# Issuing the products of y of an attention unit as one run on TensorE

## Chip, cores and metric

One core of one Trainium2 chip. The metric is the device time of one execution in microseconds, the median of the runs. The engines are TensorE (PE), VectorE (DVE), ScalarE (ACT), GpSimd (POOL) and SyncE (SP), which issues most of the DMAs.

## What is computed

A linear recurrence per batch (4) and head (8) over 768 steps with head size 48, and behind it an expert layer on its output:

```python
for t in range(S):
    S_re, S_im = a_re*S_re - a_im*S_im + k v^T, a_re*S_im + a_im*S_re   # a normalised to |a| <= 0.999
    y[:, :, t] = q @ S_re
x = y as (3072 tokens, 384)
act = x @ w_skip > 0;  e = argmax(x @ w_gate);  g = its softmax weight
out = x + g * (relu(x @ w1[e]) @ w2[e])  for the tokens with act, else x
```

All in float32; F = 1024, 8 experts.

## The kernel before

The sequence is cut into 6 chunks of 128 steps, two chunks to a group (3 groups). Three kinds of work run beside each other up to about 360 us:

- `gates` and `chain`: DVE forms the running products W of the normalised `a`, step by step (L413 and L422), for both chunks of a group at once. This is one long dependent chain on DVE and ends with the third group.
- `consumers` (`consume`, `final`): from W they scale q and k. This needs sums on PE (L496) of squares made by ACT (L482), logarithm and exponential on ACT (L503, L504), and several DVE steps (L506 to L514); `trans` turns the results on PE (L629), ACT copies them (L636). The second group is spilled to DRAM and turned back later by `turn` (PE L568, ACT L570). `wfinal` turns the state of W at the end of a group (ACT L642 and L644, PE L647, ACT L649).
- `units`: one unit per chunk c and batch b, written (c,b), 24 in all. `unit_at` multiplies k with q on PE (`pa`, L687). `unit` masks this on DVE into `at` in two halves of four heads (L710, the second is `at_ins`). For c > 0 there is a state from the chunk before: DVE makes RX (L721, L722 or L725), PE sums it (L736, L737) and ACT copies it into `Sb`, the tile `st` (L739); in chunks 4 and 5 DVE makes `st` instead (L733). Then PE adds k v^T for the next state (L746), which ACT (L753) or DVE (L751) copies into T, read by the unit of the next chunk and the same batch.

The output y of a unit is `py`, one PSUM bank (the pool has one buffer): for each of four pairs of heads, two products of `vt_` with `at` (L757) and, for c > 0, two products of `Sb` with q (L760) accumulated onto them. Each product gives 64 output partitions and is two PE instructions in the profile, so a unit with a state has 32, one without 16. ACT copies `py` into `yT` (L763), PE turns it and computes the router's scores in the same product (`px`, L771), ACT copies this to `xa` and `lg` (L778 to L789), SP stores `xa` (L793). The routing (`route`, `route1`) is done on DVE with small PE products; POOL scatters the tokens by expert (L865).

The experts (`moe`) follow from about 362 us: for each expert a first layer (L1177), ACT and DVE steps (L1179, L1180) and a second layer (L1209 to L1211), while the weights of the next expert are loaded (L1090) and split (L1101, L1102).

The order of instructions on each engine is not the order of the source. `Order` interleaves the generators above with estimated costs to get a program order; the framework's scheduler then simulates the engines and, whenever one is free, gives it the ready instruction with the lowest number in program order. A `with self.tc.high_priority(offset=n)` makes the number of what it holds smaller by n. `issue_after` keeps an instruction behind another on its own engine; `behind` adds a dependency with a wait. On the chip each engine runs its instructions in the order so fixed.

Of the kernel before, what the change touches and what calls it, by code (L numbers as in the profile page):

```python
# [19 lines left out]
B, H, S, D = 4, 8, 768, 48  # L20
# [19 lines left out]
BIG = float(1 << 20)  # L40
NEAR, ENDS = 2, 3 * LP


P_SOON, P_UNIT, P_ROUTE, P_CONSUME, P_REST, P_GATE, P_WEIGHTS = 0.4, 0.5, 0.7, 1, 1, 2, 3

# [67 lines left out]
class Kern:  # L113
# [99 lines left out]
            nc.sync.dma_start(self.xs[k * ZR:(k + 1) * ZR].rearrange("(n p) d -> p n d", p=128),  # L213
                              self.z.rearrange("p (o d) -> p o d", o=1).to_broadcast([128, ZR // 128, XW]))

    def behind(self, ins, others):

        dep = mybir.DependencyInfo(mybir.DependencyClass.Sync, mybir.DependencyReason.DATA)
        for x in others:
            self.tc.add_manual_dep(ins, x.name, dep, reason="rows of the token tables")  # L220


    def load(self, g, dst, src3, side, j0, n, off, eng=None):
# [472 lines left out]
    def unit(self, c, b):  # L696
        nc = self.nc
        V, A, PE = nc.vector, nc.scalar, nc.tensor
        nm = f"{c}_{b}"
        vt_ = self.vts[(c * B + b) % len(self.vts)]  # L700
        KT, QT = self.kqt.pop((c, b))
        o = self.order
        at = self.un.tile([128, H, C], F32, name=f"at_{nm}", tag="at")
# [26 lines left out]
        if c > 0:  # L730
            Sb = self.sts[(c * B + b) % len(self.sts)]
# [20 lines left out]
            else:  # L752
                A.copy(self.T[b], ps)  # L753
        py = self.ps_y.tile([128, H // 2, C], F32, name=f"py_{nm}", tag="py")
        for hp in range(H // 2):
            for j in range(2):
                PE.matmul(py[j * 64:j * 64 + 64, hp], vt_[:, 2 * hp + j], at[:, 2 * hp + j], start=True, stop=(c == 0))  # L757
            if c > 0:
                for j in range(2):
                    self.py_ins[b] = PE.matmul(py[j * 64:j * 64 + 64, hp], Sb[:, 2 * hp + j], QT(2 * hp + j),  # L760
                                               start=False, stop=True).ins
        yT = self.un.tile([128, H // 2, C], F32, name=f"yT_{nm}", tag="yT", bufs=1)
        self.yT_ins = A.copy(yT.rearrange("p a (k t) -> p a k t", k=2),  # L763
                             py.rearrange("p a (k t) -> p a k t", k=2)[:, :, :, ::-1]).ins
# [21 lines left out]
        ins = A.copy(xa[:, 0:DM].rearrange("p (a k) -> p a k", k=2 * D), px[:, :, 0:2 * D]).ins  # L786
# [645 lines left out]
```

## Time and profile before

| | |
|---|---|
| median of 3 runs | 508.67 us (508.4 to 509.84) |
| profiled execution | 510.8 us, span 509.1 us |
| busy in the span: PE, DVE, ACT, POOL | 424.7, 401.3, 302.7, 97.7 us |
| mean granted clock of PE | 0.895 |
| instructions at L757 and L760 | 384 and 320 |

Durations below come from the profiled execution, whose span leaves 1.7 us of its time outside. In a timeline a row is one group of equal instructions in a row on an engine: start, length from the first start to the last end, engine, line, operation, output and inputs, shapes, count. Since PE instructions are pipelined, the time that a group takes of PE is read from its start to the start of the next group.

### The profile page before, as it was taken

The numbers are of one execution on the slowest core, as the hardware profiler recorded it, in microseconds if no ns is written. First come the engines' busy times: TensorE is split into PE (matmuls) and PEld (weight loads), VectorE is DVE, ScalarE is ACT, GpSimd is POOL, SyncE is SP. The second block draws the span as 40 slices with busy tenths as digits, with TensorE's granted clock in tenths as the row PEclk, the third lists the DMA queues.
The fourth block names the chain that finished last, engine by engine and source line by source line (L and its number), as shares of the span: only waits on it lengthen the run. The fifth ranks groups of instructions, "written<-read, shape, count | busy, mean of one in ns | idle before, by whom it ended". The sixth has DMA issues, their size and how long they took to land. (4 is left out here: it accounts for less than half of the span.)

```text
span 509.1 us, 10059 instructions
## 1 busy us (share of the span) xinstructions
PE 424.7 (83%) x3294; PEld 370.8 (73%) x3294; DVE 401.3 (79%) x1009; ACT 302.7 (59%) x702; POOL 97.7 (19%) x170
## 2 busy tenths in 40 slices
PE   0345556399899878699999999999999999999992
PEld 0234324269786658478888889988989999999992
DVE  3899897989999599699899965888778666776630
ACT  5768777665567566486799663333547454755420
POOL 4011111011212222035100120333301211221111
PEclk9966655579999755799999999999999999999998
DMA  5557877588889797677786518676798667765300
GB/s 96 114 110 155 210 168 169 122 206 210 205 196 224 180 219 165 158 158 198 171 183 162 125 50 262 155 209 179 219 293 269 200 212 258 231 184 198 107 22 27
DMA packets 163457, 88.83 MB, mean 174 GB/s; under 512 B 136923, under 2 KB 156876, under 8 KB 163399
## 3 DMA queue, kind: packets, MB, share of 16 engines
q1 hardware_dynamic: 156087, 71.30, 56.0%
q0 software_dynamic: 6224, 16.63, 11.6%
q8 instruction: 28, 0.46, 0.4%
q10 hardware_dynamic: 1088, 0.20, 0.2%
q14 instruction: 30, 0.25, 0.2%
HBM read 63.39 MB, written 26.58 MB: 177 GB/s over the span
## 5 line engine op out<-in xcount | busy, mean ns | idle before, releaser
L413 DVE TENSOR_TENSOR X<-W,ain 128x192 f32<-128x192 f32 x192 | 67.8, 353 | 3.5 <-ACT ain L339 0.2
L496 PE MATMUL sw<-ws,ident 128*128 128x384 f32 x84 | 46.0, 687 | 29.3 <-ACT ws L482 29.3
L1102 DVE TENSOR_TENSOR l<-r,h 128x768 fp32r<-128x768 f32 (+1 forms) x53 | 56.5, 1072 | 12.4 <-ACT h L1101 12.3
L1179 ACT ACTIVATE hh<-ph 128x240 fp32r<-128x240 f32 x64 | 23.8, 374 | 54.6 <-PE ph L1177 54.6
L1101 ACT CAST h<-r 128x768 fp32r<-128x768 f32 (+1 forms) x53 | 49.1, 935 | 8.2 <-DMA r<-in_moe_w_dram 8.0
L422 DVE TENSOR_TENSOR W<-X 128x96 f32<-128x96 f32 x192 | 48.7, 254 | 3.6
L1177 PE MATMUL ph<-xh,l 128*128 128x240 f32 x192 | 51.2, 275 | 0.0
L496 PEld LDWEIGHTS sw<-ws,ident 128*128 128x128 f32 x84 | 20.1, 262 | 42.4 <-ACT ws L482 31.4
L1177 PE MATMUL ph<-xh,h 128*128 128x240 f32 x192 | 49.9, 275 | 0.1
L1177 PE MATMUL ph<-xl,h 128*128 128x240 f32 x192 | 49.5, 276 | 0.2 <-DVE xl L1131 0.2
L629 PE MATMUL tp<-ident,iw 128*96 128x128 f32 x128 | 24.0, 340 | 28.1 <-DVE iw L514 24.1
L636 ACT COPY qk<-tp 96x256 f32<-96x256 f32 x128 | 39.6, 369 | 8.9 <-PE tp L629 8.7
L1209 PE MATMUL po<-h,hh 128*120 128x384 f32 x128 | 43.5, 340 | 0.5 <-ACT hh L1179 0.4
L1210 PE MATMUL po<-l,hh 128*120 128x384 f32 x128 | 42.9, 337 | 0.0
L629 PEld LDWEIGHTS tp<-ident,iw 128*96 128x96 f32 x128 | 18.5, 159 | 33.0 <-issue 10.8
L757 PE MATMUL py<-at,vt 128*64 128x128 f32 x384 | 41.1, 285 | 1.3 <-DMA vt<-in_v_dram 1.3
L1211 PE MATMUL po<-h,hl 128*120 128x384 f32 x128 | 41.1, 342 | 0.0
L710 DVE TENSOR_TENSOR at<-pa,mask 128x512 f32<-128x512 f32 x48 | 32.2, 683 | 8.4 <-PE pa L687 6.4
L687 PE MATMUL pa<-qk 96*128 96x128 f32 x256 | 35.5, 286 | 2.5 <-DVE at L710 2.4
L687 PEld LDWEIGHTS pa<-qk 96*128 96x128 f32 x256 | 31.5, 194 | 6.8 <-DVE at L710 3.5
L1177 PEld LDWEIGHTS ph<-xh,l 128*128 128x128 f32 x192 | 36.4, 190 | 0.0
L1180 DVE SCALAR_TENSOR_TENSOR hl<-ph,hh 128x240 fp32r<-128x240 f32 x64 | 25.7, 402 | 13.5 <-ACT hh L1179 13.3
(254 smaller groups left out, 1075.8 us busy)
## 6 DMA issues: line engine op xcount, KB each, us to landing
r<-in_moe_w_dram SPq DMA_DIRECT2D x24, 512.0 KB
r<-in_moe_w_dram SPq DMA_DIRECT2D x32, 384.0 KB
kq<-nw POOLq DMA_DIRECT2D x24, 192.0 KB, 3.5
kq<-iw POOLq DMA_DIRECT2D x24, 192.0 KB, 3.7
vt<-in_v_dram SPq DMA_DIRECT2D x24, 192.0 KB
out_dram<-xa SPq DMA_DIRECT2D x24, 192.0 KB
nat<-kq SPq DMA_DIRECT2D x6, 768.0 KB
ain<-in_a_im_dram SPq DMA_DIRECT2D x90, 48.0 KB
```

What stands on the lines that cost most here:

```text
L413: V.tensor_tensor(X, prev.unsqueeze(1).to_broadcast([128, 2, 2, D]), windows(ain[:, j]), ALU.mult)
L422: self.cins = V.tensor_tensor(W[:, j, ::-1], X[:, :, 0], X[:, :, 1], ALU.add).ins
L496: nc.tensor.matmul(sw, self.ident, ws[:, :, c], start=(c == 0), stop=(c == 1))
L629: nc.tensor.transpose(tp[:, jj], src[:, s * 4 + jj], self.ident)
L687: nc.tensor.matmul(pa[h // 4][:, h % 4], KT(h), QT(h), start=True, stop=True)
L757: PE.matmul(py[j * 64:j * 64 + 64, hp], vt_[:, 2 * hp + j], at[:, 2 * hp + j], start=True, stop=(c == 0))
L1101: nc.scalar.copy(hi[:, ks], raw)
L1102: nc.vector.tensor_tensor(lo[:, ks], raw, hi[:, ks], ALU.subtract)
L1177: pe = PE.matmul(ph, w[:, k, js], x[:, k], start=(n == 0), stop=(n == len(terms) - 1))
L1209: PE.matmul(po, hh[:, j, sl], w2h[:, j], start=(j == 0), stop=False)
L1210: PE.matmul(po, hh[:, j, sl], w2l[:, j], start=False, stop=False)
L1211: pe = PE.matmul(po, hl[:, j, sl], w2h[:, j], start=False, stop=(j == NF - 1))
```

## The change

In a unit with a state the order of the four pairs of heads is reversed, the state products of a pair come ahead of its products with `at`, and the first of them is made to wait for the second half of `at` by an added dependency. All products of y, also those of chunk 0, get a priority 400 instructions earlier. `behind` takes a reason as an argument.

```diff
+YPRIO = 400
...
-    def behind(self, ins, others):
+    def behind(self, ins, others, why="rows of the token tables"):

         dep = mybir.DependencyInfo(mybir.DependencyClass.Sync, mybir.DependencyReason.DATA)
         for x in others:
-            self.tc.add_manual_dep(ins, x.name, dep, reason="rows of the token tables")
+            self.tc.add_manual_dep(ins, x.name, dep, reason=why)
...
         py = self.ps_y.tile([128, H // 2, C], F32, name=f"py_{nm}", tag="py")
-        for hp in range(H // 2):
-            for j in range(2):
-                PE.matmul(py[j * 64:j * 64 + 64, hp], vt_[:, 2 * hp + j], at[:, 2 * hp + j], start=True, stop=(c == 0))
-            if c > 0:
-                for j in range(2):
-                    self.py_ins[b] = PE.matmul(py[j * 64:j * 64 + 64, hp], Sb[:, 2 * hp + j], QT(2 * hp + j),
-                                               start=False, stop=True).ins
+        with self.tc.high_priority(offset=YPRIO):
+            for hp in range(H // 2) if c == 0 else reversed(range(H // 2)):
+                terms = [(vt_, lambda h: at[:, h])] + ([(Sb, QT)] if c > 0 else [])
+                terms.reverse()
+                for n, (w, x) in enumerate(terms):
+                    for j in range(2):
+                        h = 2 * hp + j
+                        self.py_ins[b] = PE.matmul(py[j * 64:j * 64 + 64, hp], w[:, h], x(h),
+                                                   start=(n == 0), stop=(n == len(terms) - 1)).ins
+                        if c > 0 and n == j == 0 and hp == H // 2 - 1:
+                            self.behind(self.py_ins[b], [self.at_ins], "the unit's products run together")
```

## Rows read from the trace of the kernel before

**Rows 1.** Windows by stretch: length, busy us per engine (instructions), PEclk, DMA share, GB/s.
```profile
110.00:176.00 66.00, 62.33 (x549) 52.38 (x548) 58.53 (x140) 38.05 (x84) 12.51 (x21) 0.95 0.86 212
...
211.00:228.00 17.00, 16.07 (x147) 13.34 (x146) 16.60 (x59) 12.70 (x32) 4.25 (x5) 1.00 0.79 174
228.00:298.00 70.00, 70.00 (x611) 57.30 (x610) 63.71 (x162) 55.53 (x139) 13.20 (x20) 1.00 0.69 157
298.00:362.00 64.00, 62.98 (x693) 57.70 (x692) 48.23 (x172) 23.73 (x62) 16.95 (x18) 1.00 0.67 189
362.00:501.00 139.00, 137.20 (x1003) 135.75 (x1001) 93.06 (x162) 70.12 (x131) 22.65 (x25) 1.00 0.62 192
```

The engines in these rows are, in this order, PE, PEld, DVE, ACT and POOL.

**Rows 2.** Waits of PE from 228 to 362 us: total, times, longest.
```profile
PE px L771 <- ACT yT L763: 0.6, 1, 0.6
PE pa L687 <- DVE at L710: 0.3, 1, 0.3
```

**Rows 3.** Timelines of DVE and PE: end of the recurrence, transpose of its end state.
```profile
297.82 0.25 DVE L422 TENSOR_TENSOR W<-X 128x96 f32<-128x96 f32 x1
...
309.86 0.38 PE L647 MATMUL tpe<-ident,e 128*96 128x128 f32 x2
```

**Rows 4.** Timeline of PE: products ahead of the first and the last break.
```profile
215.94 0.44 PE L757 MATMUL py<-at,vt 128*64 128x128 f32 x4
...
329.31 0.44 PE L757 MATMUL py<-at,vt 128*64 128x128 f32 x4
```

**Rows 5.** Timeline of PE: products, transposes and an unbroken run, with their successors.
```profile
250.87 1.06 PE L687 MATMUL pa<-qkT 96*128 96x128 f32 x8
251.76 0.60 PE L629 MATMUL tp<-ident,iw 128*96 128x128 f32 x4
...
289.71 0.60 PE L629 MATMUL tp<-ident,iw 128*96 128x128 f32 x4
290.15 1.31 PE L746 MATMUL ps<-vt,nat 128*96 128x48 f32 x14
...
341.33 0.44 PE L757 MATMUL py<-at,vt 128*64 128x128 f32 x4
...
343.24 1.16 PE L687 MATMUL pa<-qk 96*128 96x128 f32 x8
```

**Rows 6.** Timeline of PE: broken runs in units (3,2) and (4,1).
```profile
293.86 0.32 PE L757 MATMUL py<-at,vt 128*64 128x128 f32 x1
...
294.88 0.64 PE L629 MATMUL tp<-ident,nw 128*96 128x128 f32 x4
295.45 0.44 PE L757 MATMUL py<-at,vt 128*64 128x128 f32 x4
...
296.48 1.08 PE L568 MATMUL tu<-ident,nat 128*96 128x128 f32 x8
...
322.84 0.44 PE L757 MATMUL py<-at,vt 128*64 128x128 f32 x4
323.20 1.16 PE L687 MATMUL pa<-qk 96*128 96x128 f32 x8
324.30 0.44 PE L760 MATMUL py<-qk,st 96*64 96x128 f32 x4
...
325.98 1.56 PE L746 MATMUL ps<-vt,nat 128*96 128x48 f32 x16
```

**Rows 7.** Timeline of DVE: a step behind the sums of L496, with the idle before it.
```profile
274.02 0.56 DVE L506 TENSOR_TENSOR ws<-sw,ws 128x384 f32<-128x384 f32 x1 [0.65 <-ACT ws L504]
```

**Rows 8.** Windows of PE alone: length, busy us (instructions), PEclk, DMA share, GB/s.
```profile
164.00:166.00 2.00, 0.66 (x8) 1.00 0.67 140
166.00:168.00 2.00, 2.00 (x19) 0.67 1.03 260
168.00:170.00 2.00, 2.00 (x19) 0.50 0.73 188
...
172.00:174.00 2.00, 2.00 (x5) 0.62 0.93 236
```

## The prediction

> **What bounds the kernel now.** I read the windows by stretch first. From 228 to 298 us TensorE (PE) is busy for all 70.00 us and VectorE (DVE) for 63.71; from 298 to 362 PE is busy 62.98 of 64 us and DVE only 48.23; from 362 to 501, in the expert part, PE is busy 137.20 of 139 us [rows 1]. So from 228 us on the work queues for PE. Between 110 and 176 us DVE with the recurrence is nearly full (58.53 of 66), and PE has gaps, so PE time saved there need not reach the end [rows 1].
>
> Busy time of PE is not proof, since ends of matmuls are modelled. So I read the waits of PE second: from 228 to 362 us it waits 0.9 us in all, on two occasions [rows 2]. Third, the end of the recurrence against PE's queue: the last W is made at 297.82 us, and the transpose of the chunk's end state (tpe, L647), which needs only two ScalarE (ACT) copies of it, is run by PE at 309.86 [rows 3]. PE is about 12 us behind at that point; whatever it saves before is saved at the end, up to that lag. What starts at 362 us starts earlier by as much: the experts' work on PE follows without a gap, and its weight loads are released by that work's own copies.
>
> Fourth, how y's products lie on PE. A unit with a state (chunks 1 to 5, 20 units) has 32 PE instructions for y, 16 at L757 and 16 at L760. In the last four units they are one run. In earlier ones the first pair of heads' L757 products come early, then other work, then the rest, and into the rest transposes (L629, L568) fall. Counted on the PE timeline from 211 us, the breaks inside such runs are, unit by unit: 1, 1, 3, 2 (chunk 2), 2, 3, 2, 2 (chunk 3), 1, 1, 1, 0 (chunk 4), none in chunk 5: 19, the first after the products of 215.94, the last after those of 329.31 [rows 4].
>
> **What a break costs.** An unbroken run of 32 takes 343.24 - 341.33 = 1.91 us to the start of what follows, 0.06 us each [rows 5]. Four L629 transposes among full-width work take 290.15 - 289.71 = 0.44 us, eight products at L687 251.76 - 250.87 = 0.89 [rows 5]. Now a broken one: 14 products, four transposes and 16 products take 296.48 - 293.86 = 2.62 us [rows 6]. Thirty products at 0.06 are 1.79, the transposes 0.44; the break costs 0.39. Another: four products, eight of L687 and 28 products take 325.98 - 322.84 = 3.14 us [rows 6], against 1.91 + 0.89; the break costs 0.34.
>
> The Trainium skill, page TensorEngine Tiling (Array Packing), section Tiling Modes, says that changing the tiling mode drains TensorE. That would be one drain out of the half-width products and one back per break, and nothing else. The rows carry more than the two switches: after a switch the first steps of the following group are longer too, so I count the whole stretch, as above, and not the switches alone.
>
> **The change, part by part.** *Order within the run.* State product first, pairs of heads backwards: as many instructions, the same operands, the same sizes. Zero. *Hold.* The first state product also waits for the second mask product of DVE (L710). Nothing of y can then be issued while a factor is missing, so the early pair vanishes. *Priority.* The run ranks 400 instructions earlier, some two units, counting what a unit and the recurrence beside it issue, so the scheduler should put it whole onto PE at the moment that both factors are there, and transposes, L746, L687 and the sums of L496 wait up to 1.91 us longer. No DMA is added or moved by itself; the stores of xa and the scatters behind px follow their unit, so on SyncE's and GpSimd's queues nothing changes its order except by that.
>
> *What it removes.* Of the 19 breaks I leave out the two of units (2,0) and (2,1), since PE was not full before 228 us (16.07 of 17) [rows 1]. Of the other 17, 11 are around transposes, at 0.39, and 6 around L746 or L687, at 0.34: 4.3 + 2.0 = 6.3 us. The four breaks of chunk 1 lie before 176 us, where DVE is the cover: zero, at most 4 x 0.39 = 1.6.
>
> *What it adds.* Standing at the head of PE's queue just when its inputs should be ready, the run can make PE wait for a late DVE or ACT, with everything behind it waiting too. The trace has no such wait for a held run. The nearest row is px (L771), which the scheduler already puts right behind the ACT copy that it needs: 15 of them from 228 to 362 us wait 0.6 us together [rows 2], 0.04 each. For 16 units from chunk 2 on this is 0.6 us. Below: zero. Above: each as long as the one long wait of px, 16 x 0.6 = 9.6 us. I take 0.6 us, as the same kind of step in the same stretch.
>
> *What is late next.* L746 and with it the copy of T: T is read four units later, no loss. For chunk 0 (priority without hold) the first half of the products may run before the second: at most 0.39 in each of two more units, under DVE's cover, zero. The tail of chunk 5 has no break; there only px of one unit and y of the next change places, and PE is full either way.
>
> *Can the other engines follow?* From 228 to 298 us DVE has 63.71 us of work; of its 6.29 idle some is waiting for PE, so some 4 us of shortening nearly fill it, and PE's lag of 12 us [rows 3] carries what DVE cannot.
>
> **Sum.** -6.3 + 0.6 = -5.7 us. The profiled execution took 510.8 us (span 509.1), 2.1 above the median of three runs; it would come to 505.1. On the median, 508.67 - 5.7 = **503.0 us**.
>
> **Rivals.** *Only the tail counts (no measurable change).* If DVE and not PE sets the pace up to the end of the recurrence, or the scheduler still lets older transposes into the runs, then of the savings only the part after 298 us, or only the early pairs, remain. After it are 5 breaks ((3,3) two, (4,0) to (4,2) three): 1.8 - 0.6 = 1.2, **507.5**. For it: DVE at 63.71 of 70 us [rows 1]. Against: PE's lag. If the runs stay broken except for the early pairs, 6 x 0.34 - 0.6 = 1.4, 507.3, the same case.
>
> *The boosted run holds up the recurrence (slower).* In chunks 1 to 3 the sums of L496 and the products of L687 stand behind y by up to 1.91 us; DVE's order is fixed, so a late sum stops the recurrence behind it. The trace has such a wait: L506 idles 0.65 us for ACT's copy behind L496 [rows 7]. One more of these in each of 12 units costs 7.8 us against 5.7 gained: **510.8**. The break-even is 0.48 us per unit, and from 0.6 it is slower by more than 0.3%. For: DVE is nearly full up to 298 us, and the scheduler's times are not the chip's. Against: 12 us of lag on PE mean that L496 already waits its turn there, and DVE has other work.
>
> *The clock falls (smaller gain).* At 164 to 166 us PE was busy 0.66 of 2.00 us; the granted clock was 1.00 there, then 0.67, 0.50 and, in 172 to 174, 0.62, while PE was busy throughout [rows 8]. That is about 6.8 us at half clock (1.2 instead of 2.4 GHz), 3.4 us lost. A hold that leaves PE idle for so long could do it once between 228 and 362: 503.0 + 3.4 = **506.4**. Against: the waits of 0.6 and 0.3 us left the clock at 1.00 from 298 to 362 [rows 1, 2]. The Trainium skill, TensorE: Matmul & The Clock Gate, section on oscillation, warns of the same: gaps between bursts throttle the array, which speaks against holding products back; the trace agrees at 164 us and shows no fall for short waits.
>
> **How the numbers follow.** A measurement of this kernel can tell about 0.3% from no change: 507.1 to 510.2. Forecast 0.54, clock 0.06, tail only 0.17, held-up recurrence 0.23. So faster 0.60, same 0.17, slower 0.23. The low end takes all 19 breaks and the 4 of chunk 1 at 0.39 and no waits: 508.7 - 9.0 = 499.7. The high end takes in the slower rival, 511.0. Beyond it lie the upper bound of the waits (508.67 - 6.3 + 9.6 = 512.0) and larger shifts of order; I leave them and the low side with under 0.2.
>
> **What would show it.** Right: y's products are single runs of 32 of about 1.9 us, state product first, in all 20 units; the stretch from the third unit of chunk 2 to the first L1177 shortens by over 5 us; PE's waits there stay under 2 us; 362 to 501 keeps its length. Wrong: runs still broken; new PE waits on DVE L710 or ACT's copy of the state; the last W later than 297.8 us; a granted clock under 1.00 after 211 us. If the runs are whole and the stretch no shorter, PE was not the bound there. If PE's stretch shortens and the experts start no earlier, routing or weights took its place.

## The result and the profile after

The changed kernel takes 515.68 us in the median (514.52 to 523.31, 4 runs), the one before 508.53 us beside it on the same chip: **1.0128 times as long, 95% interval 1.0095 to 1.0162**. The ratio leaves out the run of 523.31 us, in a slower state into which some executions fall whatever the kernel. The forecast was 503.0 us. 515.68 lies above the range as well.

What the change says, it does: y's products lie on TensorE (PE) as one run of 32 instructions, state product first, in all 20 units with a state. The stretches after, to be held against [rows 1], have PE, PEld, DVE, ACT and POOL in that order behind the length, then the granted clock:

```profile
110.00:176.00 66.00, 60.02 (x554) 50.66 (x554) 62.64 (x153) 41.15 (x91) 16.00 (x29) 0.97 0.87 214
211.00:228.00 17.00, 14.54 (x113) 10.59 (x111) 16.93 (x58) 9.07 (x24) 1.29 (x3) 0.90 0.64 145
228.00:298.00 70.00, 69.08 (x639) 59.12 (x640) 61.44 (x159) 56.77 (x143) 15.10 (x22) 1.00 0.69 162
298.00:362.00 64.00, 59.19 (x643) 55.44 (x642) 44.49 (x145) 21.89 (x57) 14.85 (x16) 0.95 0.61 173
```

PE was full from 298 to 362 us before; now it idles 4.8 of 64 us there, at a mean clock of 0.95. Its waits from 228 to 362 us, 0.9 us in two rows before [rows 2], are now 6.0 us in eight; three of them:

```profile
PE ps L748 <- DMA nat<-kql: 1.5, 1, 1.5
PE px L777 <- ACT yT L769: 1.5, 1, 1.5
...
PE py L764 <- ACT yT L769: 0.7, 1, 0.7
```

Fixed stretches hide where the loss is, since the work moves through their borders. So I cut each trace at three events: the first instruction of px of unit (2,0), that of px of (3,3), and the first instruction of the experts (L1177 before, L1183 after). Call the parts **head, middle and tail**. The windows of the kernel before, profiled execution of 510.8 us:

```profile
0.00:221.60 221.60, 149.05 (x958) 116.16 (x959) 190.16 (x498) 147.72 (x357) 40.15 (x103) 0.77 0.74 168
221.60:309.00 87.40, 86.47 (x751) 70.57 (x750) 73.23 (x187) 67.36 (x173) 18.51 (x27) 1.00 0.67 153
309.00:361.70 52.70, 51.68 (x588) 48.00 (x587) 44.57 (x164) 17.21 (x44) 15.07 (x15) 1.00 0.76 213
```

And after:

```profile
0.00:228.10 228.10, 147.88 (x974) 113.77 (x974) 199.68 (x522) 152.20 (x369) 41.02 (x105) 0.79 0.74 169
228.10:306.80 78.70, 77.58 (x728) 67.01 (x729) 64.61 (x163) 62.47 (x158) 17.13 (x26) 1.00 0.64 152
306.80:366.20 59.40, 54.81 (x593) 51.47 (x591) 44.64 (x164) 17.56 (x46) 14.95 (x15) 0.94 0.69 199
```

Length less PE's busy time is PE's idle time. Busy: 287.2 before, 280.3 after, **6.9 us less**. Idle: 72.6 + 0.9 + 1.0 before, 80.2 + 1.1 + 4.6 after, **11.4 us more**. The experts begin 4.5 us later (366.2 against 361.7) and keep their length. That is less than the medians differ by, since the profiled execution before was 2.3 us above its median. The middle is 8.7 us shorter, but not all of that is gain: counted from event to event it holds 20 instructions fewer, of which 16 now run in the head and 4 in the tail. The recurrence itself ends ten us earlier than in [rows 3]:

```profile
287.81 0.26 DVE L424 TENSOR_TENSOR W<-X 128x96 f32<-128x96 f32 x1
```

**The head** (+6.5 us). PE begins chunk 2 at 209.31 us, before 210.95 (pa, L687). From there to px of (2,0) it takes 18.75 us instead of 10.6. On the timeline of PE after, between those two points:

```profile
212.11 1.06 PE L689 MATMUL pa<-qkT 96*128 96x128 f32 x8
214.53 1.16 PE L689 MATMUL pa<-qkT 96*128 96x128 f32 x8 [1.36 <-DVE at L712]
216.14 1.34 PE L738 MATMUL ps<-RX,ident 96*96 96x384 f32 x2 [0.45 <-DVE RX L727]
...
218.55 2.10 PE L498 MATMUL sw<-ws,ident 128*128 128x384 f32 x4
...
221.46 0.44 PE L764 MATMUL py<-qkT,st 96*64 96x128 f32 x4
...
225.00 1.06 PE L631 MATMUL tp<-ident,nw 128*96 128x128 f32 x8
225.89 0.81 PE L738 MATMUL ps<-RX,ident 96*96 96x384 f32 x2
...
228.06 1.14 PE L777 MATMUL px<-wg,yT 128*128 128x105 f32 x8 [0.71 <-DVE cand L935]
```

Before, the sum of the state (L736) followed pa's first 16 instructions and the eight transposes; now pa of the next unit stands ahead of it and waits 1.36 us for its buffer. The three waits here make 2.5 us. The clock then falls to half for 3.4 us (216.4 to 219.8), 1.7 us lost:

```profile
217.00:218.00 1.00, 1.00 (x3) 0.28 (x1) 1.00 (x5) 0.84 (x2) 0.00 (x0) 0.50 0.49 83
```

The rest, 3.9 us, is mostly work that now stands ahead of px: the sums at 218.55 (1.9 us to the next start, of which some 0.6 is the clock's loss again, so 1.3), the transposes at 225.00 (0.9) and the next unit's state sum at 225.89 (1.3, two starts 0.65 apart and the last as long), 3.5 together. That part comes back in the middle, which lacks it.

**The tail** (+6.7 us). PE's timeline and then ACT's around unit (5,1), whose products stand ahead of px of (5,0):

```profile
343.84 0.44 PE L764 MATMUL py<-qk,st 96*64 96x128 f32 x4
...
345.75 1.14 PE L777 MATMUL px<-wg,yT 128*128 128x105 f32 x8
...
348.52 1.14 PE L777 MATMUL px<-wg,yT 128*128 128x105 f32 x8 [1.52 <-ACT yT L769]
349.49 3.60 PE L689 MATMUL pa<-qk 96*128 96x128 f32 x16
```

```profile
346.93 0.19 ACT L784 COPY lg<-px 128x36 f32<-128x36 f32 x1 [3.34 <-PE pr L919]
347.02 0.48 ACT L791 CAST xah<-px 128x384 fp32r<-128x384 f32 x1
...
347.86 0.61 ACT L769 COPY yT<-py 128x512 f32<-128x512 f32 x1
```

PE goes on from the products of (5,1) at 345.75 us, but ACT, which goes by its own fixed order, waits for px of (5,0), copies it three times and copies yT of (5,1) only at 347.86. Those copies are 0.93 us of the delay. The rest no order of ACT could mend: `yT` has one buffer (`bufs=1` in the source), so yT of (5,1) cannot be written before px of (5,0), which begins at 345.75, has read the old one. PE stands for 1.52 us, and right behind it the clock is at half:

```profile
348.00:349.00 1.00, 0.48 (x4) 0.48 (x5) 1.00 (x4) 0.47 (x1) 0.00 (x0) 1.00 0.48 132
349.00:350.00 1.00, 1.00 (x9) 1.00 (x9) 1.00 (x3) 0.00 (x0) 0.63 (x1) 0.77 0.32 118
350.00:352.00 2.00, 2.00 (x11) 2.00 (x11) 1.56 (x5) 0.86 (x2) 1.39 (x3) 0.50 0.15 51
```

It stays at 0.50 to 356 us, in all for 6.8 us, 3.4 us lost: pa takes 3.40 us to the start of what follows, and the run of (5,2) 3.50 instead of 1.91. With the 1.54 us for a load at 312.39, for which PE did not wait before [rows 2], and the 0.74 us for the one bank of `py`, PE idles 3.6 us more in the tail and is busy 3.1 us more. The second trace of the changed kernel has the same waits (1.35 us in the head, 1.65, 0.74 and 1.51 in the tail); there the half clock of the tail lasts 3.4 us, and the tail is 57.9 us long.

### The profile page after: what moved, and what is told of

Read it like the earlier page. It is cut to its first block, busy times and chain, and to the rows that moved or that the text cites. A ratio compares the mean times of both kernels' runs of the same rounds, so it can differ in the third digit from the quotient of the medians.

```text
span 513.6 us, 10047 instructions
## 1 busy us (share of the span) xinstructions
PE 417.6 (81%) x3294; PEld 368.3 (72%) x3294; DVE 401.6 (78%) x1009; ACT 302.6 (59%) x702; POOL 96.9 (19%) x170
## 5 line engine op out<-in xcount | busy, mean ns | idle before, releaser
L498 PE MATMUL sw<-ws,ident 128*128 128x384 f32 x84 | 45.2, 674 | 25.6 <-ACT ws L484 25.6
L1107 ACT CAST h<-r 128x768 fp32r<-128x768 f32 (+1 forms) x53 | 49.2, 936 | 10.4 <-DMA r<-in_moe_w_dram 10.1
L1183 PE MATMUL ph<-xh,l 128*128 128x240 f32 x192 | 51.2, 275 | 0.0
L1183 PE MATMUL ph<-xh,h 128*128 128x240 f32 x192 | 49.8, 275 | 0.1
L1183 PE MATMUL ph<-xl,h 128*128 128x240 f32 x192 | 49.5, 276 | 0.2 <-DVE xl L1137 0.2
L498 PEld LDWEIGHTS sw<-ws,ident 128*128 128x128 f32 x84 | 20.0, 262 | 37.4 <-ACT ws L484 27.7
L764 PE MATMUL py<-at,vt 128*64 128x128 f32 x384 | 36.8, 279 | 1.0 <-DMA vt<-in_v_dram 0.6
L1183 PEld LDWEIGHTS ph<-xh,l 128*128 128x128 f32 x192 | 36.3, 189 | 0.0
```

What stands on the lines that cost most here:

```text
L498: nc.tensor.matmul(sw, self.ident, ws[:, :, c], start=(c == 0), stop=(c == 1))
L1107: nc.scalar.copy(hi[:, ks], raw)
L1183: pe = PE.matmul(ph, w[:, k, js], x[:, k], start=(n == 0), stop=(n == len(terms) - 1))
```

## The experiments

The theories: **A**, the loss is the order that the higher priority makes in the tail; **B**, it is the late start of chunk 2; **C**, the priority costs wherever it acts, whole runs gain; **D**, the hold costs; **E, F, G**, whatever is gained comes back as waits later (E for the recurrence, F for the tail, G for the middle itself). The chips differ: the kernel before takes 507.8 to 508.9 us on some and 519.0 to 519.3 on two others, so each ratio is against the kernel before on the same chip.

| run | edit | before there | ratio, 95% interval | head, middle, tail in its trace |
|---|---|---|---|---|
| the kernel before, three traces | | | 1 | 219.6 to 221.6, 87.4 to 87.6, 52.7 to 53.1 |
| the changed kernel, two traces | | 508.5 | 1.0128 [1.0095, 1.0162] | 228.1, 78.7, 59.4 and 228.3, 78.7, 57.9 |
| a0_after_again | none | 507.8 | 1.0139 [1.0072, 1.0205] | (the second of these) |
| e3_no_priority | no priority | 507.8 | 1.0033 [0.9992, 1.0074] | 218.5, 85.0, 54.7 |
| e7_priority_alone | old order, no hold | 507.8 | 1.0152 [1.0085, 1.0220] | 227.1, 81.8, 58.5 |
| e8_prio_c2c3 | priority in chunks 2, 3 | 508.0 | 1.0099 [1.0062, 1.0137] | 222.4, 87.0, 58.6 |
| e9_prio_c1 | priority in chunk 1 | 508.0 | 1.0057 [1.0020, 1.0094] | 220.4, 86.7, 55.4 |
| e2b_prio_c4c5 | priority in chunks 4, 5 | 508.0 | 1.0068 [1.0036, 1.0100] | 218.3, 85.2, 56.9 |
| e16_order_c2c3 | no priority, order and hold in 2, 3 | 508.9 | 0.9988 [0.9959, 1.0017] | 218.1, 87.0, 54.6 |
| e17_order_c3 | the same in 3 | 508.9 | 1.0011 [0.9975, 1.0046] | 217.8, 87.4, 53.7 |
| e13_early_only | the same in 1 to 3 | 519.0 | 1.0010 [0.9982, 1.0038] | 221.0, 89.3, 58.3 |
| e14_no_hold | no priority, no hold | 519.0 | 1.0071 [1.0042, 1.0099] | 221.0, 87.5, 63.7 |
| e11_prio_60 | lift of 60 | 519.0 | 1.0432 [1.0370, 1.0495] | 229.5, 90.0, 76.8 |
| e15_pa_twice | before, pa made twice in 2, 3 | 519.0 | 1.0201 [1.0148, 1.0254] | 222.6, 98.3, 59.4 |
| e1_prio_c1to3 | priority in chunks 0 to 3 | 519.3 | 1.0233 [1.0189, 1.0277] | 228.1, 86.1, 70.2 |
| e2_prio_c4c5 | priority in chunks 4, 5 | 519.3 | 1.0110 [1.0061, 1.0159] | 219.8, 89.3, 65.6 |
| e4_px_prio | px lifted too | 519.3 | 1.0221 [1.0172, 1.0269] | 228.0, 84.1, 67.6 |
| e5_yT_prio | copy of yT lifted too | 519.3 | 1.0241 [1.0185, 1.0296] | 227.2, 83.6, 69.0 |

### Where the priority costs, first try

```
-        with self.tc.high_priority(offset=YPRIO):
+        with self.tc.high_priority(offset=YPRIO) if not late else ExitStack():   # e1
+        with self.tc.high_priority(offset=YPRIO) if late else ExitStack():       # e2
```

and, with the products lifted as in the changed kernel,

```
+        with self.tc.high_priority(offset=YPRIO) if late else ExitStack():       # e4
+            for hp in range(H // 2):
                 pe = PE.matmul(px[:, hp], yT[:, hp], self.wg[:, hp], start=True, stop=True)
...
+        with self.tc.high_priority(offset=YPRIO) if late else ExitStack():       # e5
+            self.yT_ins = A.copy(yT.rearrange("p a (k t) -> p a k t", k=2),
```

`late` is chunks 4 and 5.

> The priority is kept for chunks 0 to 3 and taken away from chunks 4 and 5 (order of the products and hold stay everywhere). Theory A, the tail: in the changed kernel the products of unit (b+1) go ahead of px of unit b, ScalarE then copies yT late, TensorE idles 1.5 us before px of (5,1) and 0.7 us before y of (4,3), and its clock is halved from 349.4 to 356.4 us (3.5 us lost), 5.7 us in all; then this kernel takes about 510 us, with no such wait and a clock of 1.00 after 300 us. Theory B, the head: the late start of chunk 2 (first products of y at 221.5 instead of 215.9 us) is what costs; then it stays at 514 to 516 us.

> The priority only for chunks 4 and 5 (order and hold stay everywhere). Theory A: the tail's waits and the fall of the clock are there, about 5.7 us on top of the kernel before, 513 to 515 us. Theory B: no cost in the tail, 508 to 509.5 us. If order and hold alone cost something, it shows on top of either.

> The changed kernel, but in chunks 4 and 5 px has the same priority as the products of y, so that px of unit b comes ahead of y of unit b+1 again. Theory A: the waits before px and y in the tail go, the clock stays at 1.00, about 510 us. Theory B: no change against the changed kernel, 514 to 516 us.

> The changed kernel, but in chunks 4 and 5 ScalarE's copy yT has the priority too, so that on ScalarE yT of (5,1) comes ahead of the copies behind px of (5,0); on TensorE y of a unit still goes ahead of px of the unit before. Theory A with ScalarE's order as the link: the idle of 1.5 us before px of (5,1) and the half clock behind it go, the 0.7 us before y of (4,3) stays, 510 to 511.5 us. If the order of y and px on TensorE costs by itself (each px later, and the route behind it), it stays over 513 us.

These ran on a chip where the kernel before takes 519.3 us. Neither theory holds alone: the early chunks cost 1.0233, the late ones 1.0110. The head is 228.1 us with priority in the early chunks and 219.8 without, so the late start of chunk 2 is the priority's. Mending one instruction of the tail (e4, e5) brought nothing that these runs can tell, though the changed kernel was not run beside them. Their traces still have px waiting in the tail, 1.7 and 1.3 us for the copy of yT in e4 and 1.5 us for another copy of ACT in e5, and on this chip they hold waits of another kind (last section); so e4 and e5 settle nothing.

### Priority without the rest, the rest without priority

```
-        with self.tc.high_priority(offset=YPRIO):
+        with ExitStack():                             # e3, in the changed kernel
...
+        with self.tc.high_priority(offset=400):       # e7, around the old loop of the kernel before
```

> The kernel before, unchanged, for its own profile on the chip of these four runs: the earlier four runs fell on a chip where it took 519.3 us instead of 508.5, and there is no trace of it from there. By both theories below it is 1.00 of itself. If the long stretches at half clock after 215 us and the waits of the TensorE that are put down to no engine, both seen in the four earlier traces, belong to that chip, they are in this trace too (if it is the same chip); if they come from the changed order, this trace has none of them.

> The changed kernel, unchanged, beside the others on one chip. Ratio to before 1.010 to 1.016 where the chip is as the first; 1.02 to 1.03 if the chip is the one of the four earlier runs and head and tail add up (1.011 for the tail alone and 1.023 for the head alone were measured there).

> The products of y state first and held for both factors, but with the program's own priority instead of a higher one. The order of the instructions has whole runs in 13 of the 20 units with a state, and 7 breaks instead of 23. Theory C (the higher priority costs, by the order it gives to the units around the products; whole runs by themselves gain): ratio 0.985 to 0.997, with px of (5,0) and (5,1) not behind the next unit's products. Theory D (the hold costs: TensorE and the ScalarE copy behind it get y later, whatever the priority): ratio 1.005 to 1.02, with waits at y's products or at px of over 3 us between 228 and 362.

> The kernel before with the higher priority alone: y's products in their old order, not held. 17 breaks instead of 23. Theory C: slower than before, ratio 1.005 to 1.02, with experts later than before against the last write of the recurrence. Theory D: 0.99 to 1.00.

The chip was one of the quicker ones (before 507.8 us), and the trace of the kernel before has neither half clock after 215 us nor waits for no engine. Priority alone costs as much as the whole change (1.0152 against 1.0139); order and hold without it cost nothing that can be told (1.0033, interval from 0.9992). So **the higher priority is the loss**, as theory C has it. Its other half, the gain of whole runs, did not come: 0.985 to 0.997 was expected. Theory D falls by its waits more than by its ratio: the interval of e3 reaches to 1.0074, but y and px wait 1.5 us in all between 228 and 362 us, not over 3.

e7 also shows how to misread the middle: it is 5.6 us shorter there (81.8 against 87.4) in a kernel as slow as the changed one. Its runs are still broken, 7 breaks in the middle instead of 15, and about half of what shortened it is again work moved ahead of a late start (732 instructions in it instead of 751). Its tail has the changed kernel's wait too, px 1.52 us for the copy of yT at 349.71 us, here with the clock at 1.00.

### By place

These start from e3, the changed kernel without priority:

```
-        with ExitStack():
+        with self.tc.high_priority(offset=YPRIO) if c in (2, 3) else ExitStack():   # e8
+        with self.tc.high_priority(offset=YPRIO) if c == 1 else ExitStack():        # e9
+        with self.tc.high_priority(offset=YPRIO) if late else ExitStack():          # e2 once more
```

> Products whole and held everywhere, the higher priority in chunks 2 and 3 alone (the stretch on which the forecast rested); chunks 1, 4 and 5 as in the run without priority. Theory C by place (the priority pays in chunks 2 and 3, where TensorE is full, and costs in chunk 1 and in the tail): px of (2,0) near 218.5 us as without priority, the way from there to px of (3,3) near 79 us as in the changed kernel instead of 85 to 87, the tail from there to the experts 53 to 55 us; ratio 0.980 to 0.990. Theory E (whatever the recurrence gains, the tail gives back, since chunks 4 and 5 wait for the copies and loads that start at their own times): px of (3,3) early, near 298 us, but the tail 57 us and more; ratio 0.995 to 1.005.

> Products whole and held everywhere, the higher priority in chunk 1 alone. Theory C by place: the first products of chunk 2 come late (px of (2,0) at 226 us and later, against 218.5 without priority), and the ratio is 1.005 to 1.015 with the tail as without priority. Theory E: the late start is made up by the experts or earlier; ratio 0.998 to 1.004.

> The kernel of the second earlier run again (higher priority in chunks 4 and 5 alone), on the chip of these three. There it took 1.011 of before, on a chip whose traces show waits for no engine. Theory C by place: ratio 1.008 to 1.015, with px of (2,0) and (3,3) as without priority and the tail 57 us and more. Theory E: the tail is no longer than without priority (55 us), ratio 1.000 to 1.005.

Each of the three is above 1 by its own interval, e8 most; against e3 (1.0033) the intervals still touch. Even where PE is full (e8) the priority does not pay, so that half of theory C was wrong. Nor does it make the head late from one place: 220.4 us with chunk 1 (226 and more was expected) and 222.4 with chunks 2 and 3, against 228.1 with chunks 0 to 3 (e1). It takes more than one of these places; which was not taken apart. The cleanest pair is e2b against e3: head and middle agree within 0.2 us, and then the tail is 56.9 instead of 54.7. The timeline of PE in e2b has the change's own pattern, some five us earlier:

```profile
341.11 1.14 PE L777 MATMUL px<-wg,yT 128*128 128x105 f32 x8
...
343.87 1.98 PE L777 MATMUL px<-wg,yT 128*128 128x105 f32 x8 [1.51 <-ACT yT L769]
345.64 2.80 PE L689 MATMUL pa<-qk 96*128 96x128 f32 x16
```

In e3 the longest wait of the tail is 0.7 us, and the clock stays at 1.00 there. The profiled execution of e8 (517.5 us) is one of its longer ones and has two falls of the clock after 215 us, both behind its head, so its middle and tail are not used. But it shows a wait that the lift made on a load, and the clock behind it:

```profile
227.27 3.22 PE L570 MATMUL tu<-ident,nat 128*96 128x128 f32 x16 [3.01 <-DMA nat<-kq]
```

```profile
224.00:228.00 4.00, 0.99 (x10) 0.77 (x9) 4.00 (x10) 1.13 (x5) 3.10 (x3) 1.00 1.18 278
228.00:232.00 4.00, 3.88 (x20) 3.34 (x19) 3.22 (x8) 2.96 (x5) 3.33 (x3) 0.57 0.80 189
```

### Why whole runs give nothing

e13 keeps order and hold of e3 in chunks 1 to 3 alone, e14 is e3 without the hold, e11 is the changed kernel with `YPRIO = 60`; e15 is the kernel before with

```
-        for h in range(H):
+        for h in (h for h in range(H) for _ in range(2 if c in (2, 3) else 1)):
             nc.tensor.matmul(pa[h // 4][:, h % 4], KT(h), QT(h), start=True, stop=True)
```

and in e13 and e14

```
-                terms.reverse()
+                if not late:                 # e13; its hold has "and not late" too
+                    terms.reverse()
...
-                        if c > 0 and n == j == 0 and hp == H // 2 - 1:                    # e14
-                            self.behind(self.py_ins[b], [self.at_ins], "the unit's products run together")
```

> No higher priority; products state first and held in chunks 1 to 3, and in chunks 4 and 5 the old order and no hold. Theory C by place, in its last form (the priority is the loss; state first and held gains up to 3 us before the tail and gives some 2 us of it back in the tail, where px of (3,3) to the experts took 54.7 us against 52.9 before): the tail is 53 us again and the ratio 0.990 to 0.998. Theory F (a tail that begins earlier is longer whatever the order in it, because the loads and the copies keep their times): tail 54 to 56 us, ratio 0.998 to 1.005.

> No higher priority, state first everywhere, but not held for the masked factor. Chunk 3 has 10 runs instead of 9 and chunk 4 stays whole. If the hold costs (a product that waits for the masked factor keeps back what stands behind it, such as the 0.4 to 0.6 us waits for the state seen without priority), ratio 0.988 to 0.997. If it costs nothing, the same as without priority, 1.000 to 1.005.

> The kernel before with the 8 attention products of each unit of chunks 2 and 3 made twice into the same place (the result is the same): 64 products more at some 0.12 us, 7.8 us of TensorE's time in the stretch where it is full. If TensorE's work there sets the end (the step on which the forecast rested), +7 to +9 us: ratio 1.014 to 1.018. If the recurrence and the copies between the products set it, and the full TensorE only fills their gaps, +0 to +4 us: 1.000 to 1.008.

> The changed kernel with a lift of 60 places instead of 400. Its runs are whole but for 4 breaks. Theory C: a smaller lift passes less other work, so less is late: ratio 1.000 to 1.010. If any lift costs as much (the products then stand ahead of all that their own unit still has to do), 1.012 to 1.016.

This was another of the slower chips (519.0). e15 is the plainest. In the expectation its work is mis-sized: each product is two instructions, so 128 are added, 96 of them in the middle and the rest in the head, where PE is not full. In the middle, L687 alone, the kernel before (third trace) and e15:

```profile
219.60:307.20 87.60, 12.74 (x96) 11.66 (x96) 1.00 0.67 153
```

```profile
222.60:320.90 98.30, 23.71 (x192) 22.51 (x192) 1.00 0.53 124
```

11.0 us of work added, the middle 10.7 us longer. The two traces are of different chips: 1.6 us of e15's middle are waits that only its chip has (last section), and eight other instructions, some 1.7 us, have left it, so the fair pair is 9.1 us longer for 9.3 us of work. The ratio of 1.0201, 10.4 us, is of one chip. So PE does set the pace of the middle when work is **added**, nearly in full. e14 shows that the hold is not what takes the gain: without it the kernel is no faster than before (1.0071, above what was expected either way: 0.988 to 0.997 if the hold costs, 1.000 to 1.005 if not). Nor does the old order in the tail bring the gain out (e13, 1.0010): the tail is 58.3 us there, longer than either theory had it, with waits of 1.75 us for the routing and 1.03 us for yT. With a lift of 60 the kernel is slower still (1.0432); with 400, e4 and e5 took 1.0221 and 1.0241 on the other slower chip, and the changed kernel itself was run on neither. So, as far as these compare, a smaller lift does not cost less. What in its order does it was not taken apart.

### Whole runs in the full stretch alone

```
-            for hp in range(H // 2) if c == 0 else reversed(range(H // 2)):
+            for hp in range(H // 2) if c == 0 else (reversed(range(H // 2)) if c in (2, 3) else range(H // 2)):
...
+                if c in (2, 3):
                 terms.reverse()
...
-                        if c > 0 and n == j == 0 and hp == H // 2 - 1:
+                        if c in (2, 3) and n == j == 0 and hp == H // 2 - 1:
```

for e16, with `c == 3` for e17, both without priority.

> No higher priority; products state first and held in chunks 2 and 3 alone, where TensorE is full; chunks 0, 1, 4 and 5 written as before, so the order of the instructions up to chunk 2 is that of before. Breaks in the runs of chunks 2 and 3: 6 instead of 17. Theory C by place, in its last form: head and tail as before (px of (2,0) at 221 us on a chip as the first; 53 us from px of (3,3) to the experts), and the way between them shorter by 3 to 4 us (11 breaks at 0.2 to 0.4 us): ratio 0.991 to 0.996. Theory G (what the runs save comes back as waits in the same stretch, since the scheduler fills the freed places with other instructions): the way as long as before within 1.5 us, or the tail longer by as much: 0.998 to 1.006.

> The same in chunk 3 alone: 4 breaks there instead of 9, 13 instead of 17 in chunks 2 to 4 and the rest of the order nearer still to that of before. Theory C by place: 1 to 2 us shorter, ratio 0.995 to 0.999. Theory G: 0.999 to 1.006.

> The kernel before once more, for its own profile on the chip of these three runs. The times of its parts (px of (2,0), px of (3,3), the experts) are to be compared with those of the two others. If this is a slow chip (519 us), its trace shows whether the waits of TensorE for no engine that the changed kernels had there are in the kernel before too: then they belong to the chip.

Here the middle of before and of e16 hold the same 751 instructions, 15 breaks in the one and 6 in the other (the expectation says 17 for chunks 2 and 3; by the trace they have 16, one of them in the head). Middle and tail of the kernel before on that chip, then of e16:

```profile
219.60:307.20 87.60, 86.38 (x751) 70.70 (x750) 73.31 (x188) 67.58 (x173) 18.54 (x27) 1.00 0.67 153
307.20:360.30 53.10, 51.70 (x589) 48.01 (x587) 44.60 (x164) 17.24 (x44) 15.06 (x15) 1.00 0.74 213
```

```profile
218.10:305.10 87.00, 84.58 (x751) 70.19 (x749) 74.02 (x188) 66.83 (x173) 18.53 (x27) 1.00 0.64 150
305.10:359.70 54.60, 52.04 (x588) 48.04 (x587) 44.58 (x164) 17.20 (x44) 16.56 (x15) 1.00 0.74 214
```

PE's busy time in the middle falls by 1.80 us, 0.20 us for each of the nine breaks. Its idle time there rises from 1.22 to 2.42. In the tail it rises from 1.40 to 2.56. Middle and tail together: 140.7 us before, 141.6 in e16. That is theory G, and the ratio 0.9988 with an interval of 0.9959 to 1.0017 agrees. The interval alone would leave room for 2 us of gain; that the 1.80 us came back as waits rests on one trace of each. e17 says the same (1.0011). In e16's waits the added idle time lies with px behind the copy of yT (0.9 us, before 0.6), with the routing's product behind DVE (0.9), with y behind the masked factor (0.5), with L748 behind its load (0.5) and with RX (0.4): five different partners, each with a wait too short to matter alone.

No version here beats the kernel before by an amount that these runs can tell.

## Why the prediction was wrong

**The step that failed is "What it adds", 0.6 us, with "What is late next" behind it**, above all its sentence on the tail: "there only px of one unit and y of the next change places, and PE is full either way". px and y did change places, and PE was not full. The places changed on PE alone: ACT kept its order, so yT of the one waited for the other's px, which has to read the one buffer of yT first, and for its copies; PE waited 1.52 us, and the clock fell for some seven us. I had priced the hold by the 15 rows of px that do not wait [rows 2]; those rows are of an order in which the scheduler had placed each px to suit. A lift of 400 places undoes just that placing, so its price could not be read from rows of the old one. From the start of chunk 2 to the experts the account is, in us: waits in the head 2.5, idle time more in middle and tail 3.8, clock 1.7 in the head and 3.4 in the tail, 11.4 lost. Against it stand 5.3 gained, nearly all in the middle: PE's busy time there is 8.9 less, of which 3.9 only moved (3.5 to the head, 0.4 to the tail). That makes +6.1, and chunk 2 starts 1.6 earlier: the +4.5 of the experts. The term of 0.6 was in truth 11.4: 6.3 of waits and 5.1 of clock behind two of them. Its upper bound of 9.6 was for the waits alone.

**The covers.** Everything before 228 us I had at zero, with DVE as cover. For chunk 1 that holds: PE reaches chunk 2 no later (209.31 against 210.95). It fails for units (2,0) and (2,1), where the head ends 6.5 us later; some 3.5 of these are work that the middle then lacks.

**The size of a break.** 6.3 us for 17 breaks [rows 4] was somewhat too much, and this is not the step that failed. In the changed kernel the middle gained some 5 us by 15 breaks, 0.33 each, near the 0.39 and 0.34 of [rows 5, 6]; where the stretch holds the same instructions (e16), nine breaks take 1.8 us, 0.20 each. I had measured what a group loses around a break and took all of it as saved. Why e16 saves less per break stays open. The Trainium skill, page TensorEngine Tiling (Array Packing), section Tiling Modes, has TensorE drained at each change of mode, by which a break less is two drains less; that fits a saving in kind. No run here separates a drain from the rest.

**The bound.** "PE full" was right, and e15 shows it: 11.0 us added made the middle 10.7 longer. What did not follow is the other direction. With 0.9 us of waits in the whole stretch I took PE's lag of 12 us [rows 3] as the room to gain. The lag was room for the recurrence, which indeed ended 10 us sooner. For the units it was not: as e16's waits read, y's copy, px, the masks and the loads of the last chunks come hardly sooner than PE needs them, so 1 to 2 us saved meet the next wait (e3, e16, e17). No run takes one of these partners out.

**The rivals.** The sign was that of the held-up recurrence, but not its mechanism: L498 and the recurrence behind it were not late. The falling clock came true, as part of the loss and not as a smaller gain: after the waits at 214.5 and 347.0 us in the changed kernel. The Trainium skill, TensorE: Matmul & The Clock Gate, section on HAM oscillation, has waits between groups of matmuls bring the slow clock back; the rows agree at 348 us, after a wait shorter than those of its example, and at 224 us in e8, while after the 1.54 us at 312.39 the clock stayed at 1.00. "Only the tail counts" fits what order and hold do without priority (1.0033), for another reason than the one given.

**What would show it.** My test "the stretch shortens by over 5 us" was met (87.4 to 78.7) and meant little, since instructions had left the stretch; e7 meets it with broken runs. The tests that told were those on PE's waits (under 2 us; 6.0 from 228 to 362) and on the clock (1.00 after 211 us; half speed twice).

## What to carry to other kernels

A full engine with few waits says what more work there would cost, not what less work would give: before counting a saving, ask which chain runs at the same pace beside it, and how soon it would make the engine wait. A priority on one instruction group reorders one engine against others whose order stays as it was, so price it by the first partner that still serves the old order (here ACT's three copies, and the single buffers of `yT` and `py`), and try the edit without the priority. And compare stretches between the same events with the same instruction counts, or moved work looks like saved work.

## What the runs showed of the hardware

On the two chips where the kernel before takes 519 us, PE has waits for which the profile shows no releaser; on the others there were none. In e1 (the order of the changed kernel up to chunk 3) and in e15 (made from the kernel before):

```profile
PE tu L570 <- issue: 4.2, 2, 3.4
PE py L764 <- issue: 2.8, 6, 0.8
PE ph L1183 <- issue: 2.0, 1, 2.0
```

```profile
PE tu L568 <- issue: 1.6, 3, 0.8
...
PE ph L1177 <- issue: 1.2, 1, 1.2
```

The transposes of `turn` (L570, L568 in e15) and the first expert product have them in every trace from there, so they go with the chip, though the kernel before itself has no trace there. Most of the changed orders have more of them, some inside the runs of y; with priority in chunks 4 and 5 alone the ratio was 1.0110 there against 1.0068 elsewhere, with intervals that overlap. What makes them stays open. The same waits of PE do not always take the clock down: 1.36, 1.51, 1.52 and 3.01 us were followed by half speed; 1.54 at 312.39 us was not, nor 1.52 in e7.
